# The seam between two layers of a hedgehog-attention and mish network: PE's order by hand, and other tiles for the values' weights

## The chip, the cores and the metric

The kernel runs on one core of a Trainium2 chip. The metric is the device time of one execution in microseconds (us), as the median of several runs. The engines are the tensor engine (PE, with its weight loads as PEld), VectorE (DVE), ScalarE (ACT), GpSimd (POOL) and SyncE (SP), whose queue issues all transfers between the device's memory and the on-chip memory. Each engine runs its own instructions in order and waits on semaphores for the others.

## The reference

Two layers are run one after the other, with the same weights. Each is a linear attention with a learned feature map, and then a dense block with the mish activation, both behind a normalization and added to their input. S = 2048 rows, D = 640, 32 heads of 20, F = 1536, all in float32.

```python
def _A_ref(x, wqkv, w_phi, wo):
    qkv = (x @ wqkv) ...                       # q, k, v by head
    pq = einsum("bhsd,hdf->bhsf", q, w_phi);  pk = the same of k
    phi_q = concatenate([softmax(pq), softmax(-pq)]);  phi_k = the same of pk
    kv = einsum("bhsf,bhsd->bhfd", phi_k, v);  z = phi_k summed over the rows
    o = (phi_q kv) / (phi_q z + 1e-6)
    return o @ wo
def _B_ref(x, w1, b1, w2):
    h = x @ w1 + b1
    return (h * tanh(softplus(h))) @ w2
for _ in range(2):
    x = x + _A_ref(layernorm(x), A_wqkv, A_w_phi, A_wo)
    x = x + _B_ref(layernorm(x), B_w1, B_b1, B_w2)
```

## The kernel before

**Numbers.** Every large product is made of three: an operand is split into a high part (a copy on ACT in the PE's reduced float32 format) and a low part (the difference, on DVE or POOL), and high x high, high x low and low x high are added up in a PSUM bank. `split` (lines 141 to 144) does it for the values' weights: line 143 is the copy on ACT, line 144 the subtraction on DVE. `Transposed.step` (line 317 on) does it for the transposed, normalized x: the copy is `xth` (through the helper `act`, line 128), the subtraction is line 332, `xtl`. A projection (`project` and `project_half`, product on line 416) multiplies, for a row tile t and a column half c, the five slices k of x by the five slices of the weights: 3 x 5 = 15 products for one (t, c).

**Blocks.** The 2048 rows are 8 blocks (NB) of two row tiles (BT) of 128 rows. The attention has a first pass over the blocks (`attend_first`: keys, values and queries of each row tile, and the sums of keys times values in the bank `kva`), and a second pass (`attend_second`). Then `dense` runs the blocks through the dense layers: `hidden(b, pr)` makes two of the 12 slices of the hidden layer (line 941) and their mish (lines 954 to 967, on ACT, DVE and POOL; the high part of the result is line 966, the low part line 967, on POOL), and `contract(b, pr)` multiplies them by the second weights (line 981, 24 products), two steps behind (SKEW). `end(b)` adds the result to x (line 1026), takes the statistics, writes x out (line 1032), normalizes, transposes the rows in blocks and spills them to memory (line 388), from where layer 1 loads them as x (line 396).

**The seam.** At the end of layer 0's `dense`, the last `hidden(7, 5)` makes its mish in two halves (j = 0, 1). Behind its exponentials stand, in program order, the split of layer 1's first x (`nxt.all()`; its raw data lie in two v tiles and a row tile) and `load_v_weights`: five slices of the values' weights are fetched (line 138) and split into the tiles r1, in the order V_ORDER = 0, 1, 4, 2, 3. The last contraction and `end(7)` follow. Then `attend_first` of layer 1 loads the weights of the keys (line 213) and queries (line 207) that layer 0 had spilled, and runs the first block in the order v0, k0, k1, v1, q0, q1 (a letter and a row tile). On most engines the framework's planner sets the order, with modelled times and the program's order as the priority; `tc.manual_schedule(engines=...)` fixes the traced order for the engines named, and `tc.issue_after(i)` puts instructions behind i in their engine's queue.

**Tiles.** Each kind of tile has a fixed number of buffers, which are taken in turn and free when the last user of the earlier content is done: x tiles (2 buffers of two rows of 640), row tiles (name xn, 4), v tiles (2), big tiles (5), the banks `one` (4) and the double banks `mm` (2). The fetches of the values' weights take, for k = 0 to 4: row, row, v, v, big. The first values of layer 1 take four `one` banks, the last contraction both `mm`, and the keys after them take `mm` again.

Of the kernel before, what the change touches and what calls it, by code (L numbers as in the profile page):

```python
# [10 lines left out]
AF = mybir.ActivationFunctionType  # L11
# [5 lines left out]
P = 128  # L17
S = 2048
D = 640
F = 1536  # L20
H = 32
DH = 20
KD = D // P
KF = F // P
BT = 2
BLK = BT * P
NB = S // BLK
NT = S // P
G = 11
HC = D // 2  # L30
# [7 lines left out]
SKEW = 2  # L38
V_ORDER = (0, 1, 4, 2, 3)
# [12 lines left out]
def kernel(  # L52
# [13 lines left out]
    nc = tc.nc  # L66
# [11 lines left out]
    def one_tile():  # L78
        return psum.tile([P, 512], F32, tag="one", name="one", bufs=4)
# [4 lines left out]
    def x_tile():  # L84
        return work.tile([P, BT, D], F32, tag="x", name="xt", bufs=2)
# [36 lines left out]
    def act(*args, **kw):  # L122

        if last_act[0] is None or written[0]:
            ins = nc.scalar.activation(*args, **kw)
        else:
            with tc.issue_after(last_act[0]):
                ins = nc.scalar.activation(*args, **kw)
        last_act[0] = ins.ins
# [5 lines left out]
    def staged(src, stage):  # L135

        st = stage()[:, :D]
        nc.sync.dma_start(st, src)
        return st
# [42 lines left out]

    def v_weights(ws, low=nc.vector, ahead=False):

        def fetched(k):
            return staged(wv[k * P:(k + 1) * P, :], (row_tile, row_tile, v_tile, v_tile, big_tile)[k])

        st = {}
        if ahead:
            st = {k: fetched(k) for k in V_ORDER}  # L190
            yield
        for k in V_ORDER:
            split(ws[k][0][:, D:2 * D], ws[k][1][:, D:2 * D], st[k] if ahead else fetched(k), low)
            yield
# [205 lines left out]
    def project(xts, t, ws, col, ps=None, w=HC, ks=range(KD)):  # L400

        if ps is None:
            mm = mm_tile()
            ps = [mm[:, 0], mm[:, 1], mm]
        for c in range(2):
            project_half(ps[c], xts, t, ws, col, c, ks, w=w, final=ks[-1])
        return ps
# [65 lines left out]
    def attend_first(layer, x_src, first):  # L473
# [45 lines left out]
                if b == NB - 1:  # L519
                    yield  # L520

        def values(xts, i, v):
            vv = v.rearrange("p (h d) -> p h d", d=DH + 1)
            if i < BT:
                pv = project(xts, i, kv_ws, D, [one_tile(), one_tile()], ks=V_ORDER)
                for c in range(2):
                    act(vv[:, c * H // 2:(c + 1) * H // 2, :DH],
                        pv[c][:, :HC].rearrange("p (h d) -> p h d", d=DH), AF.Copy)
            else:
                pv = project(xts, i % BT, kv_ws, D)  # L530
                act(vv[:, :, :DH].rearrange("p (c h) d -> p c h d", c=2),
                    both(pv).rearrange("p c (h d) -> p c h d", d=DH), AF.Copy)
            act(vv[:, :, DH], ident[:, :H], AF.Copy, scale=0.0, bias=1.0)
            yield

        if first is None:
            E = mybir.EngineType
            with tc.manual_schedule(engines={E.PE, E.SP, E.Activation, E.DVE, E.Pool}):
                written[0] = True
                ps = one_tile()  # L540
                for _ in range(TURNS):
                    nc.tensor.transpose(ps[:, :P], ident, ident)  # L542
                xt = x_tile()
# [140 lines left out]
                    advance()  # L684
                    pending.append(g)
        else:
            nxt, kv_ws = first
            load_k_weights(kv_ws)
            q_ws = load_q_weights()
        for b in range(0 if layer else 1, NB):  # L690
            xts = nxt
            order = ("k0", "k1", "v0", "v1", "q0", "q1")
            if b == 0:
                order = ("v0", "k0", "k1", "v1", "q0", "q1")
            elif b == 1 and layer == 0:
                order = ("k0", "q0", "k1", "v0", "q1", "v1")
            elif b == NB - 1:
                order = ("k0", "k1", "v0", "v1", "q0")
            vs = [v_tile() for _ in range(BT)]
            for n, (kind, t) in enumerate(order):  # L700
                t = int(t)
                i = b * BT + t
                if b == 0 and n == 1:
                    kva = one_tile()
                    nc.vector.memset(kva[:, :360], 0.0)
                if b == NB - 1 and n == 3:
                    loaded = {0: load(0), 1: load(1, lambda: x_tile().rearrange("p t d -> p (t d)"))}
                if b + 1 < NB:
                    if n == 0 and b == 1 and layer == 0:
                        with tc.issue_after(ready):  # L710
                            xt = fetch_normed(b + 1)
                    elif n == 0:
                        xt = fetch_normed(b + 1)
                    elif n == 2:
                        nxt = xt if layer else normed(b + 1, xt)
                    elif n > 2:
                        nxt.step()
                g = {"k": lambda: keys(xts, i, vs[t]), "q": lambda: queries(xts, i),
                     "v": lambda: values(xts, i, vs[t])}[kind]()
                if b == NB - 1 and n == 3:  # L720
                    advance()
                    next(g)
                else:
                    next(g)
                    advance()
                pending.append(g)
            if 0 < b <= KD and layer == 0:
                spill_qk_weights(kv_ws, q_ws, b - 1)
            if b == 1:
                five = make_five(KD, lambda k: wo[k * P:(k + 1) * P, :], ordered=True)  # L730
                next(five)
                o_ws = []
            elif 2 < b:
                o_ws.append(next(five))
# [192 lines left out]
    def dense(x_src, x_dst, w1s, w2s, first, last):  # L927
# [41 lines left out]
        def contract(b, pr, ah, al):  # L969
            final = last and b == NB - 1  # L970
            if pr == 0:
                blocks[b][2] = [mm_tile() for _ in range(BT)]
                if final:
                    blocks[b].append(one_tile())
            pys = blocks[b][2]

            def product(t, j, c, n):
                f = 2 * pr + j
                l, w = ((ah, 0), (ah, 1), (al, 0))[n]
                ps = blocks[b][3] if final and t == c == 1 else pys[t][:, c]  # L980
                nc.tensor.matmul(ps[:, :HC], l[:, j, t * P:(t + 1) * P], w2s[f][w][:, c * HC:(c + 1) * HC],  # L981
                                 start=(f == 0 and n == 0), stop=(f == KF - 1 and n == 2))

            order = [(t, j, c, n) for t in range(BT) for j in range(2) for c in range(2) for n in range(3)]
            if b == NB - 1 and pr == KF // 2 - 1:
                order = [(t, j, c, n) for j in range(2) for t in range(BT) for c in range(2) for n in range(3)]
            for o in order:
                product(*o)

        def contract_last(b, acts):  # L990
            pys, apart = blocks[b][2:]
# [56 lines left out]
        acts = {}  # L1048
        nxt = kv_ws = None
        for i in range(len(steps) + SKEW):  # L1050
            if i < len(steps):
                b, pr = steps[i]
                if pr == 0 and b + 1 < NB:
                    fetch_rows_of(b + 1)
                if pr == 2 and b + 1 < NB:
                    blocks[b + 1] = [fetch(x_src, b + 1), None, None]
                if pr == 3 and (b + 1 < NB or not last):
                    nxt = load_turned(n1_d[b + 1] if b + 1 < NB else n2_d[0], (v_tile, v_tile, row_tile))
                acts[i] = hidden(b, pr)
                if b == 0 and pr == n_pr - 2:  # L1060
                    with tc.issue_after(exps[0]):
                        nxt.step()
                if pr == 1 and b + 1 < NB:
                    with tc.issue_after(exps[0]):
                        normalize(b + 1, ahead, ahead)
                    spill_turned(ahead, n1_d[b + 1])
                if pr == n_pr - 1 and (b + 1 < NB or not last):
                    if b + 1 < NB:
                        blocks[b + 1][1] = nxt
                    with tc.issue_after(exps[0]):  # L1070
                        nxt.all()
            if i <= KD:
                with tc.issue_after(exps[0]):
                    w = next(last_w2)
                if i:
                    w2s[6 + i] = w
            if i == len(steps) - 1 and not last:
                with tc.issue_after(exps[0]):
                    kv_ws = load_v_weights()
            if i >= SKEW:  # L1080
                b, pr = steps[i - SKEW]
                if not last or b < NB - 1 or pr < n_pr - 2:
                    contract(b, pr, *acts.pop(i - SKEW))
                elif pr == n_pr - 1:
                    contract_last(b, {pr - 1: acts.pop(i - SKEW - 1), pr: acts.pop(i - SKEW)})
                if pr == n_pr - 1:
                    end(b)
        return nxt, kv_ws

    with tc.block(schedule_with_timeline_sim=True):  # L1090
        src, first = x, None
# [81 lines left out]
```

## Time and profile before

| | before |
|---|---|
| median of 3 runs | 1355.34 us (1354.65 to 1355.56) |
| the profiled execution, its own time | 1355.98 us |
| its span, from the first to the last instruction | 1354.1 us |
| granted PE clock, mean | 1.000 |
| PE busy | 1348.3 us |
| DVE / ACT / POOL busy | 1069.7 / 584.6 / 468.9 us |
| HBM read / written | 104.61 / 62.59 MB |

Times in the views count from the first instruction. A row of a timeline gives start, duration, engine, line, operation, output<-inputs, shape and count, and in brackets how long the engine had been idle and what released it. PE rows show a product from its start to its modelled end; products overlap, so their pace is read from the distance of their starts. A row of the list of waits gives who waited for whom, the total in us, the number of waits and the longest. A row of groups ends with the busy time, the mean duration in ns and the idle time before. A row of the windows gives the stretch, its length, and the busy time and the count of PE, PEld, DVE, ACT and POOL, then the granted clock, the busy share of the DMA engines and GB/s. The chain of waits is followed back from the last instruction and lists start, length and what it ran through. SP rows are issues of transfers; their duration holds the wait for the tile.

### The profile page before, as it was taken

How to read it: one execution, taken by the hardware profiler on the slowest of the kernel's cores; microseconds unless marked ns; L12 is line 12 of the kernel's file. 1: busy time of each engine (PE TensorE's matmuls, PEld its weight loads, DVE VectorE, ACT ScalarE, POOL GpSimd, SP SyncE). 2: the span in 40 equal slices, each digit the busy share in tenths (PEclk: the TensorE clock that was granted, in tenths of full speed). 3: DMA queues.
4: the chain of work that ended last, by engine and by line, in shares of the span. 5: the costliest groups of instructions: out<-in, count | busy, mean ns of one | idle time of the engine just before them, and what ended most of it. 6: DMA issues, size and time to landing. Idle time of an engine off the chain costs nothing.

```text
span 1354.1 us, 30937 instructions
## 1 busy us (share of the span) xinstructions
PE 1348.3 (100%) x12890; PEld 1336.8 (99%) x12890; DVE 1069.7 (79%) x1810; ACT 584.6 (43%) x1039; POOL 468.9 (35%) x357
## 2 busy tenths in 40 slices
PE   9999999999999999999999999999999999999999
PEld 9999999999999999999999999999999999999998
DVE  7988888886787888778779888888768776676775
ACT  6344444222554555445444344432236444444443
POOL 3345544444322222122225556744441211111112
PEclk9999999999999999999999999999999999999999
DMA  9623336798613543334573534468964231233200
GB/s 345 176 49 73 79 60 132 195 281 275 207 28 88 118 117 85 54 97 114 147 225 69 114 71 77 81 159 241 286 242 121 79 83 27 88 98 98 66 33 21
DMA packets 350757, 169.21 MB, mean 125 GB/s; under 512 B 287241, under 2 KB 324089, under 8 KB 350617
## 3 DMA queue, kind: packets, MB, share of 16 engines
q1 hardware_dynamic: 350617, 167.23, 46.3%
q8 instruction: 101, 1.65, 0.5%
q14 instruction: 39, 0.32, 0.1%
HBM read 104.61 MB, written 62.59 MB: 123 GB/s over the span
## 4 chain that ended last, share of the span: by engine, by line
PE 99%; DMA 1%; issue 0%; ACT 0%; DVE 0%; POOL 0%; SPq 0%; POOLq 0%
PE mm L416 28%; PE one L941 25%; PE mm L981 24%; PE one L416 13%; PE mm L801 3%; PE one L326 2%; PE one L501 2%; PE mm L273 1%; DMA v<-in_wv 1%; PE one L542 0%; PE mm L999 0%; DMA r1l<-wp_d 0%; PE one L273 0%; PE one L981 0%; PE one L801 0%; PE one L999 0%
## 5 line engine op out<-in xcount | busy, mean ns | idle before, releaser
L967 POOL TENSOR_TENSOR ol<-big,ol 128x512 fp32r<-128x512 f32 (+1 forms) x98 | 130.6, 1332 | 484.7 <-ACT ol L966 400.7
L981 PE MATMUL mm<-r2h,ol 128*128 128x320 f32 x1236 | 295.5, 309 | 0.0
L941 PE MATMUL one<-xtl,r1h 128*128 128x256 f32 x960 | 268.2, 279 | 0.0
L941 PE MATMUL one<-xth,r1l 128*128 128x256 f32 x960 | 268.0, 279 | 0.0
L941 PE MATMUL one<-xth,r1h 128*128 128x256 f32 x960 | 265.9, 279 | 0.0
L981 PEld LDWEIGHTS mm<-r2h,ol 128*128 128x128 f32 x1236 | 211.9, 188 | 0.0
L981 PE MATMUL mm<-r2l,ol 128*128 128x320 f32 x618 | 190.6, 309 | 0.0
L416 PE MATMUL mm<-r1h,xth 128*128 128x304 f32 (+1 forms) x600 | 185.1, 309 | 0.0
L416 PE MATMUL mm<-r1h,xtl 128*128 128x304 f32 (+1 forms) x600 | 183.8, 307 | 0.0
L416 PE MATMUL mm<-r1l,xth 128*128 128x304 f32 (+1 forms) x600 | 183.6, 306 | 0.0
L941 PEld LDWEIGHTS one<-xtl,r1h 128*128 128x128 f32 x960 | 180.4, 188 | 0.0
L941 PEld LDWEIGHTS one<-xth,r1l 128*128 128x128 f32 x960 | 180.4, 188 | 0.0
L941 PEld LDWEIGHTS one<-xth,r1h 128*128 128x128 f32 x960 | 179.6, 188 | 0.0
L956 DVE TENSOR_SCALAR big<-big 128x512 f32<-128x512 f32 (+1 forms) x98 | 56.3, 575 | 111.4 <-ACT big L954 111.2
L465 POOL TENSOR_TENSOR big<-big,r 128x1280 f32<-128x1280 f32 x42 | 101.4, 2419 | 69.3 <-DVE r L464 44.4
L954 ACT ACTIVATE big<-one,b1s 128x256 f32<-128x256 f32 x192 | 80.8, 467 | 91.1 <-PE one L941 90.2
L958 ACT ACTIVATE big<-big,two 128x512 f32<-128x512 f32 (+1 forms) x98 | 70.1, 716 | 115.4 <-DVE big L957 115.4
L966 ACT ACTIVATE ol<-big 128x512 fp32r<-128x512 f32 (+1 forms) x98 | 60.9, 622 | 133.5 <-DVE big L965 133.4
L981 PEld LDWEIGHTS mm<-r2l,ol 128*128 128x128 f32 x618 | 116.1, 188 | 0.0
L416 PEld LDWEIGHTS mm<-r1h,xth 128*128 128x128 f32 x600 | 112.8, 188 | 0.6
L416 PEld LDWEIGHTS mm<-r1h,xtl 128*128 128x128 f32 x600 | 112.8, 188 | 0.4
L416 PEld LDWEIGHTS mm<-r1l,xth 128*128 128x128 f32 x600 | 112.8, 188 | 0.0
(186 smaller groups left out, 3147.3 us busy)
## 6 DMA issues: line engine op xcount, KB each, us to landing
big<-e_d SPq DMA_DIRECT2D x30, 640.0 KB, 6.5
x_d<-xt SPq DMA_DIRECT2D x23, 640.0 KB, 5.1
e_d<-r SPq DMA_DIRECT2D x88, 160.0 KB, 4.0
xt<-x_d SPq DMA_DIRECT2D x22, 640.0 KB, 5.6
n_d<-xn SPq DMA_DIRECT2D x176, 80.0 KB, 2.2
xt<-in_x SPq DMA_DIRECT2D x15, 640.0 KB, 4.3
xn<-x_d SPq DMA_DIRECT2D x28, 320.0 KB, 4.2
v<-n_d SPq DMA_DIRECT2D x30, 256.0 KB, 3.4
```

Source lines behind the costliest of these rows:

```text
L326: nc.tensor.transpose(ps[:, c, t * P:(t + 1) * P], self.rows[t][:, (c0 + c) * P:(c0 + c + 1) * P], ident)
L416: nc.tensor.matmul(ps[:, :w], a[:, sl], r, start=(k == 0 and n == 0), stop=(k == final and n == end))
L465: nc.gpsimd.tensor_tensor(eg, eg, r.unsqueeze(2).to_broadcast([P, 2 * H, DH]), op=ALU.mult)
L501: nc.tensor.matmul(kva[32 * q:32 * q + DH + 1, c:c + 2 * DH], v[:, (DH + 1) * h:(DH + 1) * (h + 1)], e[:, 2 * DH * h:2 * DH * (h + 1)], st ...
L801: nc.tensor.matmul(po[c][64 * q:64 * q + 64, GW * j:GW * j + w], phs[g][:n, s0:s0 + 64], kvb[:n, g, :w], start=True, stop=True)
L941: nc.tensor.matmul(ph[:, j, :], l, r, start=(n == 0), stop=(n == 3 * KD - 1))
L954: exps[0] = nc.scalar.activation(part(ta, 0)[:, j - js.start], ph[:, j, :], AF.Exp, bias=b1s[:, 2 * pr + j:2 * pr + j + 1]).ins
L956: nc.vector.tensor_scalar_min(e, e, E_CAP)
L958: nc.scalar.activation(r, n, AF.Ln, bias=two)
L966: nc.scalar.activation(ah[:, js], n, AF.Copy)
L967: nc.gpsimd.tensor_tensor(al[:, js], n, ah[:, js].bitcast(F32), op=ALU.subtract)
L981: nc.tensor.matmul(ps[:, :HC], l[:, j, t * P:(t + 1) * P], w2s[f][w][:, c * HC:(c + 1) * HC], start=(f == 0 and n == 0), stop=(f == KF - 1 ...
```

## The change

Three things are changed, all at the seam.

- `v_weights`: where the values' weights are fetched for layer 1 (not `ahead`), slices 2 and 3 go to the two halves of one x tile (`x_half`) in place of v tiles, and slice 4 to a row tile in place of a big tile.
- `contract` of the last block's last pair in layer 0 issues nothing; it hands back two functions, one for each half j of the mish, and `dense` hands them to layer 1 with a third, `end(7)`.
- A new function, `between_layers`, runs at the head of layer 1's first block, ahead of the fetch of the next block's x, with PE's order by hand: all 30 products of v0 (slices 0, 1 and the high x of 4 for both column halves, then the high x of 2 and 3, then the low x of 2, 3, 4), the copies of v0 from its banks on ACT (`keep_values`), the first half of the last contraction (12 products; the low part of the activations last), 6 products of v1's first column half, the second half of the contraction (12), `end(7)`, and the other 9 products of v1's first half. `values` then makes only what is left: v1's second half and its copies. The loads of the keys' and queries' weights now stand ahead of `end(7)` in program order.

```diff
--- before.py
+++ after.py
@@ -182,8 +182,17 @@
 
     def v_weights(ws, low=nc.vector, ahead=False):
 
+        halves_of_x = []
+
+        def x_half():
+            if not halves_of_x:
+                xt = x_tile()
+                halves_of_x.extend(xt[:, t] for t in range(BT))
+            return halves_of_x.pop(0)
+
         def fetched(k):
-            return staged(wv[k * P:(k + 1) * P, :], (row_tile, row_tile, v_tile, v_tile, big_tile)[k])
+            home = v_tile if ahead else x_half
+            return staged(wv[k * P:(k + 1) * P, :], (row_tile, row_tile, home, home, big_tile if ahead else row_tile)[k])
 
         st = {}
         if ahead:
@@ -519,13 +528,47 @@
                 if b == NB - 1:
                     yield
 
-        def values(xts, i, v):
+        def keep_values(pv, v):
+            vv = v.rearrange("p (h d) -> p h d", d=DH + 1)
+            for c in range(2):
+                act(vv[:, c * H // 2:(c + 1) * H // 2, :DH], pv[c][:, :HC].rearrange("p (h d) -> p h d", d=DH), AF.Copy)
+
+        def between_layers(xts, v, closing):
+            ps = [one_tile(), one_tile(), one_tile()]
+
+            def products(i, seq):
+                for n, (c, k, j) in enumerate(seq):
+                    rows, w = ((xts.hs, 0), (xts.hs, 1), (xts.ls, 0))[j]
+                    nc.tensor.matmul(ps[i + c][:, :HC], rows[k][:, i // 2 * P:(i // 2 + 1) * P],
+                                     kv_ws[k][w][:, D + c * HC:D + (c + 1) * HC],
+                                     start=(k == j == 0), stop=((k, j) == last))
+
+            with tc.manual_schedule(engines={mybir.EngineType.PE}):
+                last = 4, 2
+                for c in range(2):
+                    products(0, [(c, k, j) for k in (0, 1) for j in range(3)] + [(c, 4, 0), (c, 4, 1)])
+                products(0, [(c, k, j) for c in range(2) for k in (2, 3) for j in range(2)])
+                products(0, [(c, k, 2) for k in (2, 3, 4) for c in range(2)])
+                keep_values(ps[:2], v)
+                closing[0]()
+                last = V_ORDER[-1], 2
+                rest = [(0, k, j) for k in V_ORDER for j in range(3)]
+                products(2, rest[:6])
+                closing[1]()
+                closing[2]()
+                products(2, rest[6:])
+            return [], ps[2:]
+
+        def values(xts, i, v, pv=None):
             vv = v.rearrange("p (h d) -> p h d", d=DH + 1)
             if i < BT:
-                pv = project(xts, i, kv_ws, D, [one_tile(), one_tile()], ks=V_ORDER)
-                for c in range(2):
-                    act(vv[:, c * H // 2:(c + 1) * H // 2, :DH],
-                        pv[c][:, :HC].rearrange("p (h d) -> p h d", d=DH), AF.Copy)
+                if pv is None:
+                    pv = project(xts, i, kv_ws, D, [one_tile(), one_tile()], ks=V_ORDER)
+                if len(pv) == 1:
+                    pv.append(one_tile())
+                    project_half(pv[1], xts, i, kv_ws, D, 1, V_ORDER, final=V_ORDER[-1])
+                if pv:
+                    keep_values(pv, v)
             else:
                 pv = project(xts, i % BT, kv_ws, D)
                 act(vv[:, :, :DH].rearrange("p (c h) d -> p c h d", c=2),
@@ -684,7 +727,7 @@
                     advance()
                     pending.append(g)
         else:
-            nxt, kv_ws = first
+            nxt, kv_ws, closing = first
             load_k_weights(kv_ws)
             q_ws = load_q_weights()
         for b in range(0 if layer else 1, NB):
@@ -700,6 +743,8 @@
             for n, (kind, t) in enumerate(order):
                 t = int(t)
                 i = b * BT + t
+                if b == n == 0:
+                    pvs = between_layers(xts, vs[0], closing)
                 if b == 0 and n == 1:
                     kva = one_tile()
                     nc.vector.memset(kva[:, :360], 0.0)
@@ -716,7 +761,7 @@
                     elif n > 2:
                         nxt.step()
                 g = {"k": lambda: keys(xts, i, vs[t]), "q": lambda: queries(xts, i),
-                     "v": lambda: values(xts, i, vs[t])}[kind]()
+                     "v": lambda: values(xts, i, vs[t], pvs[t] if b == 0 else None)}[kind]()
                 if b == NB - 1 and n == 3:
                     advance()
                     next(g)
@@ -981,11 +1026,14 @@
                 nc.tensor.matmul(ps[:, :HC], l[:, j, t * P:(t + 1) * P], w2s[f][w][:, c * HC:(c + 1) * HC],
                                  start=(f == 0 and n == 0), stop=(f == KF - 1 and n == 2))
 
-            order = [(t, j, c, n) for t in range(BT) for j in range(2) for c in range(2) for n in range(3)]
             if b == NB - 1 and pr == KF // 2 - 1:
-                order = [(t, j, c, n) for j in range(2) for t in range(BT) for c in range(2) for n in range(3)]
-            for o in order:
-                product(*o)
+                return [lambda j=j: [product(t, j, c, n) for ns in ((0, 1), (2,)) for t in range(BT)
+                                     for c in range(2) for n in ns] for j in range(2)]
+            for t in range(BT):
+                for j in range(2):
+                    for c in range(2):
+                        for n in range(3):
+                            product(t, j, c, n)
 
         def contract_last(b, acts):
             pys, apart = blocks[b][2:]
@@ -1080,12 +1128,12 @@
             if i >= SKEW:
                 b, pr = steps[i - SKEW]
                 if not last or b < NB - 1 or pr < n_pr - 2:
-                    contract(b, pr, *acts.pop(i - SKEW))
+                    closing = contract(b, pr, *acts.pop(i - SKEW))
                 elif pr == n_pr - 1:
                     contract_last(b, {pr - 1: acts.pop(i - SKEW - 1), pr: acts.pop(i - SKEW)})
-                if pr == n_pr - 1:
+                if pr == n_pr - 1 and (last or b < NB - 1):
                     end(b)
-        return nxt, kv_ws
+        return None if last else (nxt, kv_ws, closing + [lambda: end(NB - 1)])
 
     with tc.block(schedule_with_timeline_sim=True):
         src, first = x, None
```

## The prediction

> **What bounds the kernel now.** I read the page first: span and busy time, then the chain that ended last.
>
> ```profile
> span 1354.1 us, 30937 instructions
> PE 1348.3 (100%) x12890; PEld 1336.8 (99%) x12890; DVE 1069.7 (79%) x1810; ACT 584.6 (43%) x1039; POOL 468.9 (35%) x357
> PE 99%; DMA 1%; issue 0%; ACT 0%; DVE 0%; POOL 0%; SPq 0%; POOLq 0%
> ```
>
> The tensor engine (PE) is busy for 1348.3 of 1354.1 us, and the chain runs through it almost throughout. A change that takes no products away can win at most the 5.8 us that are left. The list of waits, held to PE, says where they are, together with the two ends of the chain:
>
> ```profile
> PE one L542 <- POOL ident masks.py:199: 1.3, 1, 1.3
> PE mm L801 <- issue: 0.8, 1, 0.8
> PE one L416 <- ACT r1h L143: 0.4, 1, 0.4
> ...
> 1.34 5.38 PE one L542 x24
> 1349.10 1.77 PE one L999 x12
> 1350.89 0.49 DVE xt L1021
> ```
>
> The head (1.34 us before the first turn of the identity) and the tail (from 1350.87 to 1354.1) are most of it, and the change touches neither. One wait is at the seam: 0.4 us, of line 416 (a projection of the values) for line 143 (the high part of a values' weight). The chain of waits says what was late there, and the timeline of PE what it cost:
>
> ```profile
> 684.16 6.93 DMA v<-in_wv
> ...
> 691.11 0.75 ACT r1h L143
> ...
> 693.20 1.32 PE one L416 x9
> ...
> 685.64 0.60 PE L416 MATMUL one<-r1h,xth 128*128 128x320 f32 x3
> ...
> 691.21 0.31 PE L416 MATMUL one<-r1h,xtl 128*128 128x320 f32 x1
> 691.90 0.71 PE L416 MATMUL one<-r1h,xth 128*128 128x320 f32 x3 [0.38 <-ACT r1h L143]
> ...
> 696.41 0.30 PE L416 MATMUL mm<-r1h,xth 128*128 128x304 f32 x1
> ```
>
> From 685.64, where the first product of layer 1's values starts, to 696.41, where the first product of its keys starts, PE runs 69 products: 30 for the values of row tile 0 (v0 below), 15 for the first column half of tile 1, and the 24 of the last contraction. Nine in a row take 1.32 us, 0.147 us each, so 69 take 10.12 us; they took 10.77. The **whole prize is 0.65 us**: between the starts at 691.21 and 691.90 there are 0.54 us too many, and in the 0.71 us of the next three another 0.11. The planner already fills the wait for the last mish with values' products, so nothing larger hides there.
>
> **Part one: other homes for the values' weights.** The transfers and the engines behind them, from the timelines of SP, ACT (ScalarE) and DVE (VectorE), and one row of the windows:
>
> ```profile
> 656.78 0.34 SPq L1032 DMA_DIRECT2D x_d<-xt  x1
> ...
> 663.03 6.49 SPq L388 DMA_DIRECT2D n_d<-xn  x8
> ...
> 671.11 0.43 SPq L138 DMA_DIRECT2D xn<-in_wv  x1
> ...
> 681.06 0.39 SPq L138 DMA_DIRECT2D big<-in_wv  x1
> ...
> 683.33 0.32 SPq L213 DMA_DIRECT2D r1l<-wp_d  x1
> 684.16 2.79 SPq L138 DMA_DIRECT2D v<-in_wv  x2
> ...
> 681.55 0.62 ACT L128 ACTIVATE xth<-v 128x512 fp32r<-128x512 f32 x1
> 682.07 1.36 ACT L143 ACTIVATE r1h<-xn 128x640 fp32r<-128x640 f32 x2
> 683.33 0.62 ACT L128 ACTIVATE xth<-v 128x512 fp32r<-128x512 f32 x1
> ...
> 685.01 0.40 ACT L966 ACTIVATE ol<-big 128x256 fp32r<-128x256 f32 x1
> 687.80 0.74 ACT L143 ACTIVATE r1h<-big 128x640 fp32r<-128x640 f32 x1 [2.39 <-DMA big<-in_wv]
> ...
> 679.36 0.42 DVE L956 TENSOR_SCALAR big<-big 128x256 f32<-128x256 f32 x1 [1.83 <-ACT big L954]
> ...
> 681.38 0.29 DVE L956 TENSOR_SCALAR big<-big 128x256 f32<-128x256 f32 x1 [0.54 <-ACT big L954]
> ...
> 685.18 0.81 DVE L144 TENSOR_TENSOR r1l<-xn,r1h 128x640 fp32r<-128x640 f32 x1
> 685.91 0.68 DVE L332 TENSOR_TENSOR xtl<-v,xth 128x512 fp32r<-128x512 f32 x1
> 686.50 0.42 DVE L332 TENSOR_TENSOR xtl<-xn,xth 128x256 fp32r<-128x256 f32 x1
> 686.84 0.42 DVE L963 SCALAR_TENSOR_TENSOR big<-big 128x256 f32<-128x256 f32 x1
> 688.57 0.83 DVE L144 TENSOR_TENSOR r1l<-big,r1h 128x640 fp32r<-128x640 f32 x1 [1.31 <-ACT r1h L143]
> ...
> 691.88 2.11 DVE L144 TENSOR_TENSOR r1l<-v,r1h 128x640 fp32r<-128x640 f32 x2 [1.69 <-ACT r1h L143]
> ...
> 679.30:694.00 14.70, 14.32 (x98) 14.05 (x97) 10.71 (x21) 7.46 (x16) 3.71 (x3) 1.00 0.84 285
> ```
>
> Weights 2 and 3 now wait for the v tiles, which the last x of layer 0 leaves only when line 332 has read them (the second starts at 685.91), and weight 4 for a big tile. After the change weights 2 and 3 go to the x tile of block 6. Its last readers are the write to memory issued at 656.78 and the normalized rows, which are spilled from 663.03, so it is free some 20 us sooner. Weight 4 takes the row tile whose spill is the second half of the eight issues from 663.03; these end at 669.5. Weight 1, which waits for the first half, is issued at 671.11; weight 4 should follow about 672 and, at the 6.93 us that the slowest took, be there by 679. SP issues the same five transfers as before, three of them earlier; that puts up to 3 x 0.39 us of issues ahead of the spill and of the loads for queries and keys (the last of the keys' is issued at 683.33). Keys start at 696.41, so a delay of 1.2 us hides in the 13 us between; it would cost what it takes beyond them. The gain of this part is the 0.65 us.
>
> **Part two: PE's order by hand.** No product is added or lost. The order is 30 of v0, 12 of the last contraction's first half, 6 of the next tile, 12 of the second half, the block's end, 9 more. Without a wait that is 685.64 + 69 x 0.147, so keys start at 695.76. What each step needs:
>
> The contraction's halves come at 690.04 and 692.68, their low parts (line 967) eight products later, at 691.2 and 693.9.
>
> ```profile
> 685.54 2.32 POOL L967 TENSOR_TENSOR ol<-big,ol 128x256 fp32r<-128x256 f32 x1 [5.92 <-issue]
> 692.23 1.07 POOL L967 TENSOR_TENSOR ol<-big,ol 128x256 fp32r<-128x256 f32 x1 [4.37 <-ACT ol L966]
> 695.14 1.56 DVE L1026 TENSOR_TENSOR xt<-mm,xt 128x640 f32<-128x640 f32 x2 [1.16 <-PE mm L981]
> ```
>
> They are there at 687.86 and 693.30 as it is, so no wait even if nothing in ACT's queue gets faster. The keys' two banks come free when line 1026 has read them, 0.78 us each; the 9 products behind the block's end last 1.32 us and cover the first, the 30 products of the first key tile the second. That costs nothing; without the cover, 0.8 us.
>
> The values themselves are the open term. The old order pulls contraction products in between when a weight is late; the hand order lets **nothing** pass before v0 is through. Its products need weight 4's low part at the 8th (685.64 + 7 x 0.147 = 686.67), weight 2 from the 17th (687.99), weight 3's low part at the 20th (688.43), the low x of tiles 2 to 4 behind that (from 689.2). All of these low parts are made on DVE, in order, together with the two halves of the last mish. The window's row counts 10.71 us of DVE work from 679.36 on; with the one gap ahead of 681.38 that is not the weights' (0.54), it cannot be through before 690.6. Two bounds for the stall s:
>
> - From below, s = 0: DVE takes the weights ahead of the mish's last three steps (3 x 0.42) and the accumulator's memset (0.36). Then all that v0 needs is there at 690.6 - 1.6 = 689.0, and if the low x comes last, its last use (685.64 + 28 x 0.147 = 689.75) isn't late.
> - From above, s = 2.2: weight 3 comes last of all, 690.6 instead of 688.43.
>
> With the order of the trace and only the gaps for transfers closed, each instruction starts 0.08 before its forerunner's end (as at 685.91). Weight 4 follows line 963 and ends at 688.0, 1.3 late; behind two mish steps of 0.34, weights 2 and 3 end at 689.4 and 690.1. The pushed products ask for weight 3 twelve later, at 689.8, another 0.3 and some signalling: s = 1.7. The planner sets DVE's order anew when the transfers come early, so neither end is given; I take the middle of 0 and 1.7, rounded up, **s = 0.9**.
>
> **Part three: evictions first.** The values of tile 0 leave their banks before the block's end instead of behind it, on ACT. PE waited for no bank at the seam (the list of waits has no such row), so this is worth nothing; ACT has 7.46 us of work in those 14.7.
>
> The sum: -0.65 + 0.9 = +0.25 us. Against the profiled execution, 1355.98 us (its span and 1.9 us around it), that is 1356.2; against the median of the runs shown, 0.64 us lower, **1355.6**. A measurement of this kernel tells 0.2% (2.7 us) from no change, so this is no change.
>
> **Rivals.**
>
> *No stall* (s up to 0.4): 1354.7 to 1355.1. For it: the hand order asks for low x last, which fits weights made first. Against it: in the trace the low x is made ahead of weights 4, 2 and 3.
>
> *Trace order* (s from 1.4 to 2.2): 1356.1 to 1356.9. For it: priorities follow the program's order, where mish and x come ahead of the weights. Against it: weights 0 and 1 passed between the two xth in ACT's queue at 682.07 already.
>
> *Weight 4 stays late*, the slower side. It is third in v0's order and needs a row tile whose spill must land first; if SP issues it behind the loads that wait for the dense weights' tiles, it lands as now or later. Landing as now, its low part ends at 689.40 instead of 686.67: s = 2.7, 1357.4, still within 0.2%. Landing like the last weight now (low part near 692.7), s = 6.0 and the time 1360.7. It counts as slower from a landing about 688.4 on, when s passes 3.4. For it: the transfers are 84% busy in that window; against it: some 9 us of room between 679 and then.
>
> The Trainium skill (TensorE: Matmul & The Clock Gate, Part 1: The HAM clock gate) speaks against such a stall beyond its own length: a window of about 3.4 us without work halves PE's clock, and as long a busy one restores it. What this kernel would show of that is its head, where 24 turns took 5.38 us, 0.224 each, against this row:
>
> ```profile
> L326 PE MATMUL one<-ident,xn 128*128 128x128 f32 x242 | 34.3, 274 | 0.0
> ```
>
> There one of that shape takes 0.142 us of the busy time; 24 x 0.082 is 2.0 us. By the rule the stall of 6.0 us would give an estimated 1362.7 in place of 1360.7.
>
> *Faster by over 0.2%* would need 2.7 us, and the seam has 0.65. Only a new plan that also shortens head or tail could do it, and neither's work is touched.
>
> **How the numbers follow.** Partial stall (the forecast, 1355.6): 0.45. No stall: 0.25. Trace order: 0.14. Weight 4 late: 0.10, of which 0.02 stays below 2.7 us. A shift of the plan elsewhere in layer 1 that costs more than 2.7 us: 0.04. Faster by over 0.2%: 0.02. So faster 0.02, same 0.45 + 0.25 + 0.14 + 0.02 = 0.86, slower 0.08 + 0.04 = 0.12. The range runs from 1354.6 (no stall, and 0.1 us for the spread) to 1357.4 (weight 4 as late as now); the forecast's own is 1355.1 to 1356.1.
>
> **What would show it.** Right: no row of PE waiting for line 143 on a transfer; the transfers of weights 2, 3 and 4 issued before 677; PE's waits in the seam for line 144 (low parts) of 0.4 to 1.4 us in total; keys starting near 696.7 (695.76 + 0.9). Keys at 695.8 make the first rival right, 697.2 to 698 the second. Wrong in the step on weight 4: its issue still behind the loads for keys. Wrong as a whole: a new wait of PE outside 685 to 697, or a time beyond 1358.1 or under 1352.6.

## The result and the profile after

| | before | after |
|---|---|---|
| median | 1355.56 us (17 runs, 1354.25 to 1356.27) | 1357.29 us (17 runs, 1356.63 to 1360.42) |
| ratio, 95% interval | | 1.0017 (1.0010 to 1.0023) |
| profiled execution, its span | 1355.98, 1354.1 us | 1357.21, 1355.4 us |

The change made the kernel slower: by 1.73 us (0.13%) in the medians, by 0.17% in the ratio of the runs, whose interval leaves no change out. The forecast was 1355.6 us, no change. The time still lies in the stated range, just under its upper end of 1357.4, but neither the loss nor its cause was what was forecast. The page of the changed kernel hardly differs from the one before (line numbers are now up to 48 higher):

```profile
span 1355.4 us, 30936 instructions
PE 1348.4 (99%) x12890; PEld 1336.8 (99%) x12890; DVE 1070.4 (79%) x1810; ACT 584.7 (43%) x1039; POOL 469.9 (35%) x357
```

PE does the same work, and the span is 1.3 us longer: PE stands still more. Its list of waits (total in us, number, longest) says where:

```profile
PE one L585 <- POOL ident masks.py:199: 1.3, 1, 1.3
PE one L510 <- POOL big L474: 1.2, 1, 1.2
PE mm L846 <- issue: 0.7, 1, 0.7
PE mm L425 <- POOL xtl L341: 0.3, 1, 0.3
```

The wait for a values' weight is gone. In its place PE waits 1.2 us in line 510, the sums of keys times values, for line 474, the normalization of the keys' features on GpSimd, and 0.3 us for a low x from the same engine. **The seam itself runs without a wait**, as its part of the chain shows (start, length, what):

```profile
685.79 4.40 PE one L542 x30
690.19 1.76 PE mm L1026 x12
691.95 0.88 PE one L542 x6
692.83 1.32 PE one L425 x9
694.15 1.76 PE mm L1026 x12
695.91 1.32 PE one L542 x9
697.23 0.88 PE one L425 x6
698.11 26.37 PE mm L425 x188
```

Line 542 is `between_layers`. Among its products stand fifteen of line 425 that it does not issue, nine ahead of the last contraction's second half and six ahead of the keys: the second half of tile 1's values. Before, they came behind both key tiles:

```profile
704.98 2.19 PE one L416 x15
```

An order by hand fixes the named products among themselves; the planner still puts others between them.

Counting PE's products from the start aligns the traces. The table gives the start of the n-th product less that of the same n in the profile of before:

| n (its start before) | after | after, again | what lies ahead of it |
|---|---|---|---|
| 6500 (680.79) | -0.01 | -0.17 | head and layer 0 |
| 7000 (736.31) | -0.66 | -0.82 | the seam |
| 7200 (748.46) | +1.26 | +1.10 | the sums of layer 1's block 1 |
| 9000 (905.36) | +1.25 | +1.10 | the rest of the first pass |

The seam gave the 0.65 us that it had in this profile, and block 1, 60 us later, took **1.92 us**: 1.22 and 0.28 us of idle time, and some 0.4 us that the list of waits doesn't show. It counts a wait only from a product's modelled end, which lies behind the start of the next one (0.31 us long, 0.147 apart).

Why GpSimd was late shows in three engines' timelines. First ACT and VectorE, after:

```profile
690.08 0.77 ACT L128 ACTIVATE v<-one 128x320 f32<-128x320 f32 x2 [2.93 <-PE one L542]
706.55 0.68 ACT L128 ACTIVATE big<-mm 128x608 f32<-128x608 f32 x1 [3.37 <-PE mm L425]
```

The row of before that answers to the second:

```profile
705.01 0.68 ACT L128 ACTIVATE big<-mm 128x608 f32<-128x608 f32 x1 [1.80 <-PE mm L416]
```

```profile
707.41 1.55 DVE L461 TENSOR_REDUCE m<-big 128x32 f32<-128x640 f32 x2 [1.06 <-ACT big L128]
...
737.56 1.50 DVE L523 STREAM_TRANSPOSE r<-r 128x1280 f32<-128x1280 f32 x1
738.99 0.51 DVE L473 RECIPROCAL r<-r 128x64 f32<-128x64 f32 x1
```

The keys of tile 1 leave their bank at 706.55, 1.54 us later than before, because fifteen values' products now go ahead of them. VectorE idles 1.06 us for them, and from there to 743 it has no gap worth naming, so the delay stays in its queue. Its plan changed too: the turn (block transpose) of the second query's features, 1.50 us, now stands ahead of the reciprocal of block 1's first key. Before, it stood behind it:

```profile
736.05 0.56 DVE L464 RECIPROCAL r<-r 128x64 f32<-128x64 f32 x1
736.88 1.51 DVE L514 STREAM_TRANSPOSE r<-r 128x1280 f32<-128x1280 f32 x1 [0.28 <-POOL r L465]
```

GpSimd follows that reciprocal. Its rows after, then before, then PE's after:

```profile
739.57 2.37 POOL L474 TENSOR_TENSOR big<-big,r 128x1280 f32<-128x1280 f32 x1 [2.17 <-DVE r L473]
741.90 1.29 POOL L341 TENSOR_TENSOR xtl<-xn,xth 128x512 fp32r<-128x512 f32 x1
743.16 2.36 POOL L474 TENSOR_TENSOR big<-big,r 128x1280 f32<-128x1280 f32 x1
```

```profile
738.07 2.37 POOL L465 TENSOR_TENSOR big<-big,r 128x1280 f32<-128x1280 f32 x1
740.39 1.30 POOL L332 TENSOR_TENSOR xtl<-xn,xth 128x512 fp32r<-128x512 f32 x1
741.65 2.37 POOL L465 TENSOR_TENSOR big<-big,r 128x1280 f32<-128x1280 f32 x1
```

```profile
745.57 0.40 PE L510 MATMUL one<-big,v 128*21 128x40 f32 x20 [1.22 <-POOL big L474]
746.25 0.41 PE L425 MATMUL mm<-r1h,xtl 128*128 128x304 f32 x1 [0.28 <-POOL xtl L341]
```

After 2.17 us of waiting GpSimd starts 1.5 us later than before, 2.16 us later if PE's lead of 0.66 us is counted, and its second key ends at 745.52 instead of 744.02. PE, which had come to that place at 744.66, is now there at about 744.3.

### The profile page after: what moved, and what is told of

Same layout as the page of the kernel before. It is cut to its first block, busy times and chain, and to the rows that moved or that the text cites. A ratio compares the mean times of both kernels' runs of the same rounds, so it can differ in the third digit from the quotient of the medians.

```text
span 1355.4 us, 30936 instructions
## 1 busy us (share of the span) xinstructions
PE 1348.4 (99%) x12890; PEld 1336.8 (99%) x12890; DVE 1070.4 (79%) x1810; ACT 584.7 (43%) x1039; POOL 469.9 (35%) x357
## 4 chain that ended last, share of the span: by engine, by line
PE 99%; POOL 0%; DVE 0%; issue 0%; ACT 0%; POOLq 0%; ACTq 0%
PE mm L425 28%; PE one L986 25%; PE mm L1026 24%; PE one L425 12%; PE mm L846 3%; PE one L335 2%; PE one L510 2%; PE mm L282 1%; PE one L542 0%; PE one L585 0%; PE mm L1047 0%; PE one L282 0%; PE one L1026 0%; PE one L846 0%; PE one L1047 0%; POOL big L474 0%
```

## The experiments

Theory A: the turn ahead of the reciprocal makes GpSimd late. Theory B: the new homes of the weights shift later transfers. Rival C: the late keys of tile 1. Each experiment changes the kernel named, and each median stands against runs of the kernel before on the same chip.

**The changed kernel again.**

> The changed kernel unaltered, for a second profile and more times. Both theories: 1.2 to 2.5 us over before. Theory A (VectorE's order in layer 1's first two blocks): the seam again without a wait, PE's only new waits at the sums of keys times values of block 1 (for the normalization of the keys' features on GpSimd) and at the products behind them, 1 to 2 us together; a slow execution has more of the same wait, at the same place. Theory B (the homes of the weights alone shift later transfers): waits on a transfer or an x tile instead.

1357.23 us against 1355.70, ratio 1.0010 (1.0002 to 1.0019). The same two waits at the same place, 1.2 and 0.3 us, and the same step of 1.92 us in the table above. The only wait for a transfer on PE's list, 0.4 us of line 282, lies at 6.1 us, in the head, and there is none for an x tile: B is out for the wait.

**The new homes alone**, on the kernel before.

```diff
...
-            return staged(..., (row_tile, row_tile, v_tile, v_tile, big_tile)[k])
+            home = v_tile if ahead else x_half
+            return staged(..., (row_tile, row_tile, home, home, big_tile if ahead else row_tile)[k])
```

> The kernel before with the new homes of the values' weights alone. Theory A: the turn of the second query stays behind the reciprocal of block 1's first key, so no wait there; the seam's 0.65 us are won with the planner's own order: 1354.7 to 1355.1, 0.4 to 0.65 under before. Theory B: the wait of about 1.2 us in block 1 is here too: 0.5 to 1.5 us over before.

1356.57 against 1355.70, 1.0006 (0.9997 to 1.0015): not A's time, and in B's range, but not by B's wait. There is no wait in block 1 (its product 7200 starts as late as 7000, +0.62 and +0.63), so B falls. But the seam isn't won: from product 6500 to 7000 it loses 0.42 us. With the weights early the planner has other values' products to place, and PE waits for the last mish and for the keys' banks:

```profile
PE mm L425 <- DVE xt L1035: 0.3, 1, 0.3
PE mm L990 <- POOL ol L976: 0.2, 1, 0.2
```

**PE's order by hand without the new homes**, the changed kernel with the old ones (the last diff the other way round). The early evictions are still in it.

> The changed kernel with the old homes (v and big tiles). Theory A: VectorE's order in blocks 0 and 1 is that of the changed kernel, so the wait in block 1 is here too, and on top the seam waits for weights 4, 2 and 3 (2.5 to 6 us, since nothing may pass them): 3 to 7 us over before, less what a later start gives the second place. Theory B: only the seam's wait, and none in block 1.

1362.29 against 1355.70, 1.0044 (1.0031 to 1.0057): both waits, as A said. From product 6500 to 7000 it loses 3.70 us, then 1.92 in block 1 as the changed kernel does. So the homes and the order are worth something only together, and the step in block 1 comes with the order by hand or with the early evictions, which this run doesn't tell apart.

**Both turns a step later**, on the changed kernel.

```diff
-            if i == NT - 3:
+            if i == NT - 3 or layer and i < BT:
                 yield
```

> The changed kernel with one step more between the normalization and the turn of block 0's two queries in layer 1, so that both turns stand behind the first key's reciprocal of block 1 on VectorE. Theory A: the wait in block 1 goes: 1354.7 to 1355.0, 0.4 to 0.65 under before. Rival C (the keys of tile 1 come 1.5 us late because PE makes the second half of tile 1's values first, and VectorE's queue never recovers): the wait shrinks by less than half, 1356.3 or more.

1354.63 against 1355.70, 0.9995 (0.9986 to 1.0004), and 2.6 us under the changed kernel of the same batch. PE's waits have no row of GpSimd's features any more, and GpSimd starts 2.9 us earlier than in the changed kernel (in this execution PE, too, is 0.5 us earlier there):

```profile
736.65 2.37 POOL L474 TENSOR_TENSOR big<-big,r 128x1280 f32<-128x1280 f32 x1
```

**One turn later**, the second query's (`layer and i == 1` in that line).

> The changed kernel with the one step more for the second query of block 0 alone: its turn (1.45 us on VectorE) goes behind the reciprocal of block 1's first key, the first query's turn stays where the changed kernel has it. Theory A (this one turn is what makes GpSimd late): the wait in block 1 falls from 1.5 us to 0.2 or less, 1354.7 to 1355.3. Rival C (late keys of tile 1): the wait stays at 1 us or more, 1356.3 or more. Rival D (both turns must move): 0.5 to 1 us of it stay.

1355.84 against 1355.80, 1.0005 (0.9996 to 1.0013). The step in block 1 falls from 1.92 to 0.78 us, and waits of 0.4 and 0.2 us are left there. That is neither A's 0.2 nor C's 1 us; it is what rival D said: both turns must move.

**The one turn early**, on the kernel before: the reciprocal of that one key is issued behind the second query's turn, and VectorE's order is otherwise untouched. The planner moved something on PE as well: twelve of the sums in block 1 come sooner.

```diff
...
-        last_recip[0] = nc.vector.reciprocal(r, r).ins
+        if behind:
+            with tc.issue_after(last_turn[0]):
+                nc.vector.reciprocal(r, r)
+        else:
+            last_recip[0] = nc.vector.reciprocal(r, r).ins
...
-                    advance()
+                    advance(bool(layer) and b == 1 and n == 3)
```

> The kernel before with the same two instructions of VectorE the other way round: the second query's turn ahead of the reciprocal of block 1's first key, all else in its order. Theory A: GpSimd begins that key's normalization about 0.9 us later (the turn ends near 738.4, the reciprocal near 738.9, instead of 738.07), and PE, which had some 0.6 us to spare at the sums of block 1, waits 0.3 to 0.9 us: 1355.9 to 1356.5 against 1355.6. Rival C: no wait, 1355.6.

1356.23 against 1355.80, 1.0007 (0.9998 to 1.0016). PE waits in block 1, and the step there is 0.65 us (from -0.77 to -0.12):

```profile
PE mm L417 <- POOL xtl L333: 0.3, 1, 0.3
PE one L506 <- POOL big L470: 0.2, 1, 0.2
```

So the turn has its price without any of the change; the median alone couldn't show it. Not all of that price is the turn's length: standing earlier, it also waits 0.87 us for GpSimd, which it didn't in the changed kernel.

**The values behind the keys**, on the changed kernel: the second half of tile 1's values is held behind the keys of tile 1 on PE.

```diff
...
+                    with tc.issue_after(last_key[0]):
                         project_half(pv[1], xts, i, kv_ws, D, 1, V_ORDER, final=V_ORDER[-1])
```

> The changed kernel with the second half of tile 1's values behind the keys of tile 1 on PE, as before. VectorE's order keeps both turns ahead of the first key's reciprocal of block 1. Theory A: a wait in block 1 stays, smaller by what VectorE no longer idles ahead of the keys (1 us at most): 0.4 to 1.5 us, 1355.4 to 1356.4. Rival C: no wait, 1354.7 to 1355.0.

1355.45 against 1355.80, 0.9999 (0.9991 to 1.0008). VectorE still takes both turns ahead of the reciprocal, yet there is no wait (the step is 0.04): C was right here about the wait (not about the time, 1354.7 to 1355.0), and A alone wrong. GpSimd starts the first key at 735.58:

```profile
735.58 2.37 POOL L475 TENSOR_TENSOR big<-big,r 128x1280 f32<-128x1280 f32 x1 [1.24 <-DVE r L474]
```

A and C are both delays in VectorE's queue ahead of one reciprocal. Before, PE had some 0.6 us to spare there; neither delay alone gives the whole wait, and taking either kind away can end it.

**Both turns later, on the kernel before**, as a control.

> The kernel before with both turns a step later, as in turns_later, and nothing else. Theory A: PE doesn't wait in block 1 in either, so no difference, 1355.3 to 1355.9. Rival E (the later turns win time by themselves, wherever they stand): 0.7 us or more under before.

1356.21 against 1355.80, 1.0005 (0.9997 to 1.0014): no gain. Later turns win nothing where no wait stood, so the rival by which they gain of themselves falls.

**The evictions back behind the block's end**, on the changed kernel; with the rest as changed. What lets the planner put the values' second half first? It needs a bank `one`. The early copies on ACT end at 690.85 (the row at 690.08), and the second half starts at 692.67; Theory F says that the one makes the other.

```diff
-                keep_values(ps[:2], v)
                 closing[0]()
...
                 closing[2]()
+                keep_values(ps[:2], v)
                 products(2, rest[6:])
```

> The changed kernel with its third part undone: the copies of tile 0's values stand behind the block's end in program order, as before; homes and PE's order by hand as in the changed kernel. Theory F (the early copies free a bank `one` early, so the planner lets PE make the second half of tile 1's values ahead of the keys, the second keys come 1.5 us late, and VectorE's queue is that much late until block 1): the second half goes back behind the keys, no wait in block 1, the seam's 0.65 us stay: 1354.7 to 1355.2. Rival: PE's order by hand or the new homes do it in another way, and the wait of 1.5 us or more stays: 1356.5 or more.

1355.06 against 1355.90, 0.9994 (0.9985 to 1.0003), and 2.2 us under both medians of the changed kernel, which are from other chips. The second half is back behind the keys, the seam is as tight as in the changed kernel (-0.67 from product 6500 to 7000), and block 1 has no wait (a step of 0.04):

```profile
686.01 4.40 PE one L542 x30
690.41 1.76 PE mm L1026 x12
692.17 0.88 PE one L542 x6
693.05 1.76 PE mm L1026 x12
694.82 1.32 PE one L542 x9
696.13 8.40 PE mm L425 x60
704.53 2.19 PE one L425 x15
```

The copies now come long after the start of the keys (695.97), and the second half behind them:

```profile
701.06 0.74 ACT L128 ACTIVATE v<-one 128x320 f32<-128x320 f32 x2
```

The part of the change that frees the values' banks early is the one that makes it slower, and through the place of the second half: with the copies as early as in the changed kernel and that half held behind the keys, the run "The values behind the keys" had no wait either. That the planner went by the free bank is read from these times; no run shows its choice itself, and the early copies alone were not tried on the kernel before.

**Both mends, and the turns once more.**

> The changed kernel with both mends, the values' second half behind the keys and both turns a step later. If the wait in block 1 is a sum of delays in one queue, either mend had already taken all of it, and both together give what turns_later gave: 1354.4 to 1355.1. If each mend moved something else as well, up to 0.5 us less.

> turns_later again, beside the other two on one chip: 0.3 to 1.2 us under before. If it is no better than before here, the first figure was luck of the executions.

1355.56, 0.9998 (0.9989 to 1.0007), and 1355.03, 0.9993 (0.9985 to 1.0002), against 1355.90. Neither has a wait in block 1 (steps of 0.03 and 0.04). The first misses its forecast of 1354.4 to 1355.1 us, the second is in its own. Once the wait is gone, nothing more is to be had there; their medians differ by less than their intervals can tell. The versions that read lowest, the turns a step later and the evictions behind the end, lie 0.8 to 1.1 us under the kernel before in their batches, and the intervals of the ratios reach 1.0002 to 1.0004: clearly under the changed kernel (by 2.6 us in the one batch that has both), under the one before only likely.

**The profiles side by side.** The table gives the start of GpSimd's normalization of block 1's first key, less what PE is ahead or behind at product 7000, so that it counts against PE's own place. Before, the second normalization ended 0.64 us before PE's sum started.

| kernel | GpSimd's start | against before | PE's wait at the sums |
|---|---|---|---|
| before | 738.07 | | none |
| changed | 740.23 | +2.16 | 1.2 |
| changed, one turn later | 738.95 | +0.88 | 0.2 |
| before, the one turn early | 738.91 | +0.84 | 0.2 |
| changed, both turns later | 737.79 | -0.28 | none |
| changed, evictions behind the end | 736.95 | -1.12 | none |
| changed, values behind the keys | 736.41 | -1.66 | none |

PE waits in just those kernels in which GpSimd is later than the 0.64 us to spare. The delays don't simply add: each of the last three versions wins back more than the 2.16 us that were lost, and VectorE's order differs in each. What each of its instructions adds is not worked out here.

## Why the prediction was wrong, point by point

- **The bound and the prize.** That PE bounds the kernel held, and the changed kernel's seam is 0.65 us shorter, as computed. But the prize was read from one execution. The two experiments that leave the seam as before, the early turn and the control, started the keys 0.49 and 0.47 us sooner by the same count and have no wait for line 143 on their lists. In the first of them, the late weight came just in time; 0.21 us lie between the starts, where the profile of before had 0.69:

```profile
690.92 0.31 PE L417 MATMUL one<-r1h,xtl 128*128 128x320 f32 x1
691.13 0.71 PE L417 MATMUL one<-r1h,xth 128*128 128x320 f32 x3
```

  So the seam was worth 0.2 us in two of the three profiles of its old form. Made against the one profile, -0.65 + 1.92 is 1.27, and the profiled executions differ by 1.23. With 0.2 us for the seam the loss would be some 1.7 us, and the medians differ by 1.73; beside the spread from elsewhere (last section) so close a match is luck.
- **Part one, homes.** Right: the transfers of weights 2 and 3 (two halves of the x tile) were issued at 663.04 and 671.51, that of weight 4 by 674.57, all ahead of 677.
- **Part two, s = 0.9.** Wrong by its size: s was 0, the lower bound and the first rival, to which I gave 0.25. ACT and VectorE took the weights ahead of the low x, which the trace of before spoke against:

```profile
684.76 1.55 DVE L144 TENSOR_TENSOR r1l<-xn,r1h 128x640 fp32r<-128x640 f32 x2
686.24 1.55 DVE L144 TENSOR_TENSOR r1l<-xt,r1h 128x640 fp32r<-128x640 f32 x2
687.71 0.68 DVE L341 TENSOR_TENSOR xtl<-v,xth 128x512 fp32r<-128x512 f32 x1
688.31 0.42 DVE L341 TENSOR_TENSOR xtl<-xn,xth 128x256 fp32r<-128x256 f32 x1
```

  The last weight's low part ends at 687.79 and was needed at 688.43; the last low x ends at 688.73 and was needed at 689.75.
- **Part three, evictions: the step that failed.** "PE waited for no bank at the seam (the list of waits has no such row), so this is worth nothing". A bank that frees early removes no wait, but the planner spends it: on the values' second half, ahead of the keys. I costed an eviction by who waits for it and not by what its bank lets in. It was worth 1.9 us of loss: the step in block 1 is 1.92 us, and 0.04 in the run that undoes this part alone.
- **The rest of the sum.** "A shift of the plan elsewhere in layer 1" stood in the list with 0.04, only for more than 2.7 us and without a mechanism. The view that would have given one was at hand in the profile of before: VectorE with two gaps of 0.3 us in all the time from 706 to 741, and GpSimd's normalization ending at 744.02 for a sum that started at 744.66. That margin of 0.64 us should have been in the prediction, with the 2.2 us of values' products that may move ahead of the keys.
- **The slower rival**, weight 4 late, did not happen in the changed kernel; the run with the old homes shows that its mechanism was real (3.70 us at the seam, of which 1.9 by the distance of PE's starts is weight 4), and that the clock can drop there (below).
- **The signs and the range.** No wait for line 143 and transfers ahead of 677 held. The sign of being wrong as a whole, a new wait of PE outside 685 to 697, came true. The start of the keys misled: 697.95 is what the second rival asked for, but fifteen more products stood ahead of them (2.2 us); without these it is 695.75, the first rival's 695.8. And the time lies in the range by luck: its upper end stood there for a late weight 4.

## What to carry to other kernels

Where one engine is busy throughout, look for the places where another engine arrives with little to spare, and test every reorder against them, also 60 us downstream: here the margin was 0.6 us, behind a queue that had two gaps of 0.3 us in 35 us in which to catch up. Freeing a buffer early is not free of charge when a planner may use it; say what it will put there and what that delays. And take a stall of a few tenths from more than one execution before counting it as a prize.

## What the runs showed of the hardware that was not expected

**The clock drops on a partial standstill.** With PE's order by hand and the old homes, PE stood still for 1.06 and 0.44 us within the 2.4 us up to 688.4, with one product between. From 688.44 its granted clock was half for 3.41 us. The timeline of PE, and the windows (stretch, length, busy time of PE, PEld, DVE, ACT, POOL, clock, DMA share, GB/s):

```profile
687.35 0.42 PE L533 MATMUL one<-r1h,xth 128*128 128x320 f32 x1 [1.06 <-ACT r1h L143]
688.22 0.47 PE L533 MATMUL one<-r1l,xth 128*128 128x320 f32 x1 [0.44 <-DVE r1l L144]
688.48 0.47 PE L533 MATMUL one<-r1h,xth 128*128 128x320 f32 x1
```

```profile
686.00:688.40 2.40, 0.89 (x4) 0.40 (x4) 1.53 (x4) 0.74 (x1) 1.05 (x1) 1.00 1.04 385
688.40:691.90 3.50, 3.28 (x12) 2.72 (x11) 1.82 (x4) 1.89 (x3) 0.73 (x1) 0.51 0.23 86
```

The products of that stretch started 0.267 us apart (688.48 to 690.62) instead of 0.147, some 1.2 us for ten of them, beside the waits themselves. The Trainium skill (TensorE: Matmul & The Clock Gate, Part 1) gives the length of that stretch, about 3.4 us, and an idle window as its cause; here the 3.41 us ahead of the drop were idle for 1.5 us in all (PE was busy for 1.90), and that was enough. In block 1 of the changed kernel 1.5 us of idle time did not do it in the two profiles, but 5 of its 28 executions had a mean clock of 0.998 or 0.999 (0.001 of 1355 us is 2.7 us at half clock), four of them among its six slowest, up to 1360.42 us. Where the clock fell in them isn't on record. Of the 87 executions of the kernel before in the three batches, 5 did.

**The entry to layer 1's second pass varies** between executions of like kernels, as time in which the profile shows no releaser: 0.7 us after (the row of line 846), and in two others of these runs

```profile
PE mm L846 <- issue: 0.2, 1, 0.2
```

```profile
PE mm L801 <- issue: 2.3, 2, 2.0
```

(both turns later on the changed kernel, and on the kernel before). From the start of product 9000 to that of 9300 the thirteen profiles range from 0.99 us less to 1.81 us more than before; the two of the changed kernel alone differ there by 0.96 us. The first 1000 products vary by 0.7 us. Elsewhere, but for the seam, block 1 and 0.7 us near the end of two of them, they agree within 0.03 us from stage to stage. What sets the entry stays open; it can blur every median above.
